# Attention turns beside an MLP stream: two turns in one round, with one stretch of projections and two groups of transposes

## The chip, the cores and the metric

The kernel runs on one core of a Trainium2 chip. The core has a matrix engine (TensorE, PE in the profile) that writes only to PSUM, a small memory of eight banks; VectorE (DVE), ScalarE (ACT) and GpSimd (POOL) for everything elementwise, of which POOL does not read PSUM in this program; and SyncE (SP), whose queue issues nearly all DMA transfers. The engines run side by side, each through its own queue in order, and wait for one another through semaphores. The metric is the device time of one execution in microseconds (us), lower is better.

## What is computed

A kernelized attention (random features), then a gated MLP on its output, all in float32:

```python
q, k, v: (8, 8, 576, 64); omega: (128, 64); x: (4608, 512); d_ff = 1536

def phi(x):
    proj = np.einsum('bhsd,md->bhsm', x, omega)
    sq = np.sum(x * x, axis=-1, keepdims=True) / 2.0
    h = proj - sq
    h = h - np.max(h, axis=-1, keepdims=True)
    return np.exp(h) / np.sqrt(m)
q_p, k_p = (phi(q_s), phi(k_s))
kv = np.einsum('bhsm,bhsd->bhmd', k_p, v)
z = np.sum(k_p, axis=2)
num = np.einsum('bhsm,bhmd->bhsd', q_p, kv)
den = np.einsum('bhsm,bhm->bhs', q_p, z)[..., None] + 1e-06
x = (num / den) with heads beside each other

g = x @ w_gate
silu = g * (1.0 / (1.0 + np.exp(-g)))
val = x @ w_val
out = silu * val @ w_out
```

## The kernel before

The attention is cut into groups of 256 rows of a pair of heads, 72 groups of q and 72 of k. A *step* holds two groups: six steps of k and k, sixty of q and k, six of q and q, 72 in all. A step passes through a pipeline of stages, one or more turns of the main loop apart:

- `st_transpose` (line 430): PE transposes the loaded rows (tile `nat`) into PSUM tile `pt`, ACT copies it to `x`; POOL squares the rows (`sq`).
- `st_project` (458): sixteen small matmuls on half of the array's rows each (`pp<-omT,x` in the profile, 64 rows by 128), into two PSUM tiles `pp`.
- `st_max` (477): DVE reduces `sq` and `pp` and works out the bias `st`; `st_exp` (497): ACT writes the features `ph` by exponentials, 128x128 at a time, and frees `pp`.
- `k_accumulate` (589): eight matmuls into `kvacc`, two turns after the projection, in two halves. When a batch's half is complete, `kv_finalize` (518) has ACT copy it to `kvr`; for batches from 4 on (`BPOOL`) PE then transposes the sums z (`zp`), ACT copies them, and they go to DRAM and back, spread over the partitions (`load_z`, 537).
- `q_transpose` (622): PE transposes q's features (`ptq`), ACT copies them to `qt`.
- For batches under 4, `q_mult` (635) multiplies with `kvr` (`po`), DVE divides (`xn`), and `q_out` (673) transposes `xn` (`xt`). From batch 4 on, the division comes first: `q_den` (550) has POOL multiply the features with z (`jk`) and DVE reduce them, `q_norm` (576) has POOL scale the features, and `q_out` does the output matmul itself (`xt<-qt,kvr`, half of the columns each). ACT (and DVE, for the first three tiles) copies `xt` out, to SBUF as a pair of high and low parts or as `xo` to DRAM.

Float32 matrix products of the MLP are made of three products of rounded parts (high and low). `stream` (772) yields the MLP's units: `g`, `v` (twelve 512-column matmuls each) and, per 128 rows, `o` (`down`, nine matmuls). Three tiles of 512 rows run through this stream in twelve visits (three tiles, four sets of three feature blocks); between two sets, new weights are fetched (`wraw`), split by ACT and POOL (`whi`, `wlo`, `split_piece`) a few units later (`land`). After a `v`, DVE multiplies with the gate (`sl`), ACT casts the result (`hh`) and POOL takes the remainder (`hl`).

The weights come in a packed form that `convert_all` (276) turns into float32 in six small steps per piece on ACT, DVE and POOL; one call of `tick` (314) issues one step, 216 in all. `behind_step` (270) keeps such work behind the newest bias of `st_max` and the newest exponential.

PSUM has eight banks: three for the MLP (`ps_moe`), two for projections (`ps_proj`), one each for `ps_att`, `ps_tr` and `kvacc`. A tile waits until the last user of its slot is done.

The main loop (line 1170) runs 76 turns. The first 25 (`EARLY`) have no MLP beside them and keep their order `CLOSE`. From turn 25 on, each turn runs the list `GROUPED` (1138): all float32 stages of PE in one group, then three `SHARE`s, then `q_norm` and `q_mult`, then three `SHARE`s. A planner has worked out beforehand how many microseconds of the MLP should be done by each turn (`course`, by its own estimates 24.4 us for a visit); at a `SHARE`, `give` takes units from the stream until its share is used up (a unit that is too long is charged to the next shares), and a part of the turn's conversion steps is issued. After the loop, the remaining six tiles go through the MLP in pairs, with nothing of the attention beside them (`pair_rounds`, line 973).

The instructions are finally put in each engine's queue by a list scheduler that goes by the order of writing but may take a later instruction when an earlier one isn't ready by its own estimate; so a queue's order can differ from the text's.

In the profile, every matmul is on line 103 and every transpose on line 107, since small helpers record them; they are told apart by tile names.

Of the kernel before, what the change touches and what calls it, by code (L numbers as in the profile page):

```python
# [24 lines left out]
def kernel(  # L25
# [295 lines left out]

    LAND = 3
    landing = []

    def load_weights(f, i):
        need(f, i)
# [2 lines left out]
    def land(upto=None):  # L329

        for t in landing:
            t[0] -= upto is None
        while landing and (landing[0][0] <= 0 or upto in [(f, i) for _, f, i, _ in landing]):
            _, f, i, raw = landing.pop(0)
            new_weights(f, i)
            with behind_step():
                split_piece(f, i, raw)
# [92 lines left out]
    def st_transpose(n):  # L430
        if n >= NS:
            return
        nat = nats.pop(n)
        pt = ps_tr(f"pt_{n}", [P, 2, G])
        for i in range(2):
            for c in range(CH):
                turned_in[:] = [
                    transpose(
                        pt[:, i, c * P : (c + 1) * P], nat[:, i, c].rearrange("p h d -> p (h d)"), ident
                    )  # L440
                ]
        x = att.tile([P, 2, G], F32, name=f"x_{n}", tag="x")

        st = att.tile([P, 4, 2, CH, 2], F32, name=f"st_{n}", tag="st", bufs=6)
# [12 lines left out]

    def st_project(n):
        if n >= NS:
            return  # L460
        x, st, sq = sts[n]

        new = ps_moe if n < EARLY and n % 2 else ps_proj
        pp = [new(f"pp{hh}_{n}", [P, 2, CH, M]) for hh in range(2)]
        for i in range(2):
            for c in range(CH):
                for hh in range(2):
                    r = slice(hh * D, (hh + 1) * D)
# [49 lines left out]
    def kv_finalize(b, a2):  # L518
        acc = kvacc.pop((b, a2))
        raw = att.tile([P, 4, VW], F32, name=f"kvr{b}_{a2}", tag="kvr", bufs=4)  # L520
        nc.scalar.copy(raw, acc)  # L521
        for j in range(2):
            kvst[b, 2 * a2 + j] = raw[:, 2 * j : 2 * j + 2, :]
        if b >= BPOOL:

            zp = ps_att(f"zp{b}_{a2}", [4, P])
            transpose(zp, raw[:, :, D], ident)
            zs = att.tile([4, P], F32, name=f"zs{b}_{a2}", tag="zs")
# [5 lines left out]
    zds = {}  # L534
    zbc = {}

    def load_z(n):
# [12 lines left out]
    def q_den(n):  # L550

        n -= JLAG
        for _, b, g, gr in slots(n, "q"):
            if b < BPOOL:
                continue
            ph = box["q", b, g].rearrange("p c (h m) -> p c h m", m=M)
            jk = att.tile([P, CH, 2, M], F32, name=f"jk{b}_{g}", tag="jx")
# [12 lines left out]
            dn = att.tile([P, 3, CH, 2], F32, name=f"dj{b}_{g}", tag="dj", bufs=6)  # L570
# [64 lines left out]
    def q_mult(n):  # L635

        n -= MLAG
        for _, b, g, gr in slots(n, "q"):
            if b >= BPOOL:
                continue  # L640
            qt = qts.pop((b, g))
            po = ps_att(f"po{b}_{g}", [P, CH, 2, VW])
            for c in range(CH):
                prs = pairs_of(gr)[c]
                w = P // len(prs) if gr is None else P
# [8 lines left out]
            dn = att.tile([P, 2, CH, 2], F32, name=f"dn{b}_{g}", tag="dn", bufs=4)  # L654
            nc.vector.tensor_scalar_add(dn[:, 0], po[:, :, :, D], EPS)
            nc.vector.reciprocal(dn[:, 1], dn[:, 0])
            xn = att.tile([P, CH, 2, D], F32, name=f"xn{b}_{g}", tag="jx")
            nc.vector.tensor_tensor(
                xn.rearrange("p c h d -> p (c h) d"),
                po[:, :, :, 0:D].rearrange("p c h d -> p (c h) d"),  # L660
# [10 lines left out]
    cols_done = [0]  # L671

    def q_out(n):
        n -= OLAG
        for i, b, g, gr in slots(n, "q"):
            po = (ps_att if n + OLAG < EARLY or i else ps_tr)(f"xt{b}_{g}", [P, G])
            first = column(b, gr)
            if b < BPOOL:
                xn = xns.pop((b, g))
# [2 lines left out]
            else:  # L682
# [3 lines left out]
                for pr, o, w in segs:  # L686
                    for hh in range(2):
                        matmul(
                            po[hh * D : (hh + 1) * D, o : o + w], kvst[b, pr][:, hh, 0:D], qt[:, hh, o : o + w],
                            start=True, stop=True, skip_group_check=True,  # L690
                        )
            j, o = tile_of(first)
            if gr is None:
                parts_ = [(po.rearrange("d (r c) -> d r c", c=RES), slice(0, NPAIR), j, o, RES)]
# [4 lines left out]
                    parts_.append((po[:, cut:G], gr[0], j + 1, 0, G - cut))  # L699
            for src, pr, j, o, w in parts_:  # L700
                if j in x_dram:
                    xo = att.tile(list(src.shape), F32, name=f"xo{b}_{g}_{j}", tag="xo", bufs=3)
                    nc.scalar.copy(xo, src)
                    nc.sync.dma_start(x_dram[j][:, pr, o : o + w], xo)
                    continue
# [7 lines left out]
        return bool(slots(n, "q"))  # L713


    def mm1(ps, wts, xs):
# [33 lines left out]

    def down(j, k_, ht, wts, next_set, tt):
        fs = sorted(ht)
        po = ps_moe(f"o{j}_{k_}_{tt}", [P, DM])
        for n, f in enumerate(fs):
            need(f, 2)
# [12 lines left out]
        if next_set is not None and tt == TILES[j][1] // P - 1:  # L768
            for f in next_set:
                load_weights(f, 2)  # L770

    def stream():

        todo = []
        for vi, (j, s_, k_) in enumerate(visits):
# [37 lines left out]
            for f in fs:  # L813
# [306 lines left out]
    def turn_next(n):  # L1120
# [17 lines left out]
    GROUPED = (  # L1138
        q_out,
        st_project,  # L1140
        q_transpose,
        lambda n: k_accumulate(n, 0),
        lambda n: k_accumulate(n, 1),
        st_max,
        st_exp,
        q_den,
        lambda n: st_transpose(n + 1),
        SHARE,
        SHARE,
        SHARE,  # L1150
        lambda n: q_norm(n + 1),
        q_mult,
        SHARE,
        SHARE,
        SHARE,
    )

    for n in range(2):
# [8 lines left out]
    warm(2, turned_in[0])  # L1167
    loaded = 3
    ends = []
    for n in range(NN):  # L1170
        if loaded <= n + LA:
            load(loaded)
            loaded += 1
# [3 lines left out]
            loaded += 1  # L1177
        if n == FIRST_RAW:
            load_raw(0)
        want = OPS * np.interp(clock[n + 1], [clock[m] for m, _ in marks], [x for _, x in marks])  # L1180
        order = CLOSE if n < EARLY else GROUPED
        left = len(order) if n < EARLY else order.count(SHARE)
        for what in order:
            with ExitStack() as es:
                if n < EARLY:
                    for ins in ends if what is st_project else ends[:1]:
                        es.enter_context(tc.issue_after(ins.ins))
                if what is not SHARE:
                    what(n)
            if n < EARLY:  # L1190
                if what is st_project:
                    ends.clear()
                ends.append(newest_pe[0])
            if what is turn_next and n < 2:
                warm(2, turned_in[0])
            if n < EARLY or what is SHARE:
                due = course[n + 1] - given[0] - debt[0]
                if due > 0:
                    give(due / left)
                for _ in range(int(np.ceil((want - ticks[0]) / left))):  # L1200
                    tick()
                left -= 1
        load_z(n)
    late.close()
    for name, pool in (
        ("win", tc.tile_pool(name="win", bufs=1)),
# [38 lines left out]
```

## Time and profile before

| what | us |
|---|---|
| median of 3 runs (1165.26 to 1167.43) | 1166.89 |
| the profiled execution | 1166.82 |
| its span, first to last instruction | 1165.0 |
| ACT busy in the span | 678.3 |
| DVE busy | 707.4 |
| POOL busy | 615.5 |
| chain of waits that ended last: share of PE | 74% |
| same chain: "issue" (no wait that the profile shows) | 2% |

A busy share says how long an engine had at least one instruction under way. Matmuls are pipelined: an instruction of 0.39 us is followed by the next after 0.23 us, so the distance from start to start is the cost, and a row "x16" of the timeline merges sixteen neighbours of the same kind. In a list of waits, "PE zp L107 <- ACT kvr L521: 2.0, 3, 1.1" means that PE, ahead of the instruction that writes zp, stood idle for 2.0 us in all, three times, at the longest 1.1, until ACT's instruction on line 521 was done.

### The profile page before, as it was taken

Reading aid. Unit: us, or ns where it says so; the run is one execution under the profiler, and the core shown is the slowest. Engines: PE = TensorE matmul, PEld = TensorE weight load, DVE = VectorE, ACT = ScalarE, POOL = GpSimd, SP = SyncE. Lnnn points to the kernel's source line nnn. Section 1 sums busy time; section 2 is a strip of 40 time slices with the busy share of each in tenths; the row PEclk is TensorE's granted clock in tenths of the full one; section 3 lists DMA queues with packets and bytes.
Section 4 is the critical chain, followed back from the end, with each engine's and each line's share of the span. In section 5 each row is a group of like instructions: output and inputs, shape, how many; then the busy total and the mean of one; then the engine's idle time right before and its main releaser. Section 6 shows DMA issues by size and latency. Waiting matters only on the chain.

```text
span 1165.0 us, 18915 instructions
## 1 busy us (share of the span) xinstructions
PE 1137.2 (98%) x6645; PEld 939.5 (81%) x6646; DVE 707.4 (61%) x1289; ACT 678.3 (58%) x1539; POOL 615.5 (53%) x559
## 2 busy tenths in 40 slices
PE   8999999999999999989999999999999999999998
PEld 6888888888878778867788778888878888888886
DVE  5787667455656656565474566665566666456654
ACT  5887886876776866757434544454544445444441
POOL 5664433344556675587245555544455543455551
PEclk9999999999999999999999999999999999999999
DMA  6764445655445642322544111124211111211103
GB/s 137 179 160 114 128 142 161 178 135 143 122 126 137 168 132 78 114 68 65 154 118 126 46 55 55 55 74 122 59 55 55 54 37 46 81 55 55 46 19 72
DMA packets 173966, 114.30 MB, mean 98 GB/s; under 512 B 125840, under 2 KB 144304, under 8 KB 173872
## 3 DMA queue, kind: packets, MB, share of 16 engines
q1 hardware_dynamic: 172528, 112.78, 35.5%
q8 instruction: 52, 0.85, 0.3%
q10 hardware_dynamic: 1344, 0.33, 0.1%
q14 instruction: 42, 0.34, 0.1%
HBM read 87.88 MB, written 25.18 MB: 97 GB/s over the span
## 4 chain that ended last, share of the span: by engine, by line
PE 74%; DVE 10%; ACT 6%; POOL 4%; DMA 3%; issue 2%; SPq 1%; ACTq 0%; POOLq 0%; DVEq 0%
PE o L103 22%; PE a L103 16%; PE c L103 8%; PE g L103 6%; PE pp L103 4%; PE v L103 4%; PE d L103 4%; PE kvacc L103 3%; ACT ph L505 3%; PE ptq L107 2%; PE po L103 2%; PE pt L107 2%; PE xt L103 1%; DVE st L490 1%; POOL wlo L264 1%
## 5 line engine op out<-in xcount | busy, mean ns | idle before, releaser
L505 ACT ACTIVATE ph<-pp,st 128x128 f32<-128x128 f32 x576 | 157.8, 386 | 26.5 <-DVE st L493 26.0
L763 DVE TENSOR_TENSOR acc<-o,acc 128x512 f32<-128x512 f32 x156 | 105.8, 684 | 94.6 <-PE o L103 94.3
L446 POOL TENSOR_TENSOR sq<-nat 128x512 f32<-128x512 f32 x72 | 78.2, 1086 | 130.5 <-DVE st L483 89.1
L950 POOL TENSOR_TENSOR wlo<-wspare,whi 128x512 fp32r<-128x512 f32 (+1 forms) x60 | 61.0, 1037 | 117.4 <-ACT whi L949 111.0
L490 DVE TENSOR_REDUCE st<-pp 128x4 f32<-128x512 f32 x144 | 92.5, 683 | 39.0 <-PE pp L103 38.7
L264 POOL TENSOR_TENSOR wlo<-wraw,whi 128x512 fp32r<-128x512 f32 x59 | 82.7, 1406 | 26.7 <-ACT whi L263 22.8
L103 PE MATMUL pp<-omT,x 64*128 64x128 f32 x1152 | 87.3, 285 | 3.2 <-ACT x L454 2.2
L103 PEld LDWEIGHTS pp<-omT,x 64*128 64x128 f32 x1152 | 72.6, 187 | 20.2 <-issue 11.2
L950 POOL TENSOR_TENSOR wlo<-s,whi 128x512 fp32r<-128x512 f32 x64 | 82.6, 1311 | 3.8 <-ACT whi L949 3.8
L1059 ACT COPY late<-a 128x512 f32<-128x512 f32 x72 | 42.2, 586 | 59.7 <-PE a L103 58.5
L103 PE MATMUL o<-whi,late 128*128 128x512 f32 x192 | 74.5, 389 | 0.0
L571 DVE TENSOR_REDUCE dj<-jk 128x4 f32<-128x512 f32 x36 | 24.6, 684 | 73.5 <-POOL jk L567 60.6
L103 PE MATMUL kvacc<-v,ph 128*128 128x65 f32 x512 | 65.9, 268 | 0.5 <-ACT kvr L521 0.5
L824 POOL TENSOR_TENSOR hl<-sl,hh 128x512 fp32r<-128x512 f32 x36 | 47.0, 1308 | 34.8 <-ACT hh L823 34.7
L103 PEld LDWEIGHTS kvacc<-v,ph 128*128 128x128 f32 x512 | 63.1, 192 | 0.8 <-ACT kvr L521 0.6
L1063 DVE TENSOR_TENSOR late<-c,late 128x512 f32<-128x512 f32 x25 | 17.3, 692 | 69.7 <-PE c L103 60.6
L103 PE MATMUL g<-xh,whi 128*128 128x512 f32 x144 | 59.4, 412 | 0.0
L103 PE MATMUL o<-whi,hh 128*128 128x512 f32 x144 | 58.5, 406 | 0.1
L303 POOL TENSOR_TENSOR wc<-st 128x512 int32<-128x512 int32 x36 | 37.5, 1042 | 39.6 <-DVE st L298 17.2
L103 PE MATMUL v<-xh,whi 128*128 128x512 f32 x144 | 57.9, 402 | 0.0
L103 PE MATMUL g<-xh,wlo 128*128 128x512 f32 x144 | 57.7, 401 | 0.0
L103 PE MATMUL g<-xl,whi 128*128 128x512 f32 x144 | 57.2, 397 | 0.0
(261 smaller groups left out, 3369.4 us busy)
## 6 DMA issues: line engine op xcount, KB each, us to landing
wraw<-wscr SPq DMA_DIRECT2D x63, 256.0 KB, 2.7
wspare<-wscr SPq DMA_DIRECT2D x60, 256.0 KB, 2.8
wscr<-wc SPq DMA_DIRECT2D x36, 256.0 KB, 2.2
out_dram<-acc SPq DMA_DIRECT2D x72, 128.0 KB, 2.4
nat<-in_k_dram SPq DMA_DIRECT2D x64, 128.0 KB, 3.0
nat<-in_q_dram SPq DMA_DIRECT2D x64, 128.0 KB, 3.1
v<-in_v_dram SPq DMA_DIRECT2D x62, 128.0 KB, 3.5
st<-in_moe_w_gate_dram SPq DMA_DIRECT2D x12, 512.0 KB, 4.1
```

The source lines that it names most:

```text
L103: newest_pe[:] = [nc.tensor.matmul(*args, **kw)]
L107: newest_pe[:] = [nc.tensor.transpose(*args, **kw)]
L264: nc.gpsimd.tensor_tensor(lo, raw, hi.bitcast(F32), op=ALU.subtract)
L303: nc.gpsimd.tensor_tensor(ui, ri, low, op=ALU.add)
L446: nc.gpsimd.tensor_tensor(sq, nat, nat, op=ALU.mult)
L490: nc.vector.tensor_reduce(st[:, 1, :, :, hh], pp[hh], axis=AX.X, op=ALU.max, negate=True)
L505: step_end["s"] = nc.scalar.activation(ph[:, c, hh * M : (hh + 1) * M], pp[hh][:, i, c, :], AF.Exp, bias=st[:, 3, i, c, hh : hh + 1], scal ...
L571: nc.vector.tensor_reduce(dn[:, 0], jk, axis=AX.X, op=ALU.add)
L763: nc.vector.tensor_tensor(a_, po, a_, op=ALU.add)
L824: nc.gpsimd.tensor_tensor(hl, h, hh.bitcast(F32), op=ALU.subtract)
L950: nc.gpsimd.tensor_tensor(lo, src_, hi.bitcast(F32), op=ALU.subtract)
L1059: newest["s"] = nc.scalar.copy(keep[name], ps)
```

## The change

From turn 25 on, the loop goes in twos. One round (`DOUBLE`) does the work of two turns, n and n+1, in this order on PE: half of `k_accumulate` of n, the output of both (`q_out_both`), the projections of n and of n+1, the other half of `k_accumulate`; six SHAREs with `q_norm` of n+1 between them; z's transposes; a half of `k_accumulate` of n+1, q's transposes of n and the rows' transposes for n+2; two SHAREs; q's transposes of n+1, the rows' transposes for n+3, the other half of `k_accumulate`; the exponentials of n+1; two SHAREs; `q_mult` of both; two SHAREs.

In the first six SHAREs of a round no conversion step is issued and no weight piece is split (`held`), unless the next unit needs it. The casts of `hh` and `hl` are no longer issued behind each `v`, but collected (`uncast`) and issued by `settle`, once in a round, or by `down` if it reads one that is still open.

PSUM slots change hands: the projections of n go to `ps_att` and `ps_tr`, those of n+1 to `ps_proj`; `xt` goes to `ps_moe`, two groups to a tile; `po` of n+1 goes to `ps_tr`; `zp` goes to `ps_moe`. Transposes `pt` stay in `ps_tr` and `ptq` in `ps_att` (a second group in `ps_tr`). In SBUF, `st` and `dj` go from six buffers to four, `xo` from three to five, `jk` and `zs` to one, and `xn` gets a tag of its own.

```diff
-        while landing and (landing[0][0] <= 0 or upto in [(f, i) for _, f, i, _ in landing]):
+        while landing and (landing[0][0] <= 0 and not held or upto in [(f, i) for _, f, i, _ in landing]):
...
-        new = ps_moe if n < EARLY and n % 2 else ps_proj
-        pp = [new(f"pp{hh}_{n}", [P, 2, CH, M]) for hh in range(2)]
+        if n < EARLY:
+            new = (ps_moe, ps_moe) if n % 2 else (ps_proj, ps_proj)
+        else:
+            new = (ps_proj, ps_proj) if (n - EARLY) % 2 else (ps_att, ps_tr)
+        pp = [new[hh](f"pp{hh}_{n}", [P, 2, CH, M]) for hh in range(2)]
...
-            zp = ps_att(f"zp{b}_{a2}", [4, P])
+            zraw[b, a2] = raw
+    def z_rows():
+        for (b, a2), raw in zraw.items():
+            zp = ps_moe(f"zp{b}_{a2}", [4, P])
             transpose(zp, raw[:, :, D], ident)
...
-            po = ps_att(f"po{b}_{g}", [P, CH, 2, VW])
+            odd = n + MLAG >= EARLY and (n + MLAG - EARLY) % 2
+            po = (ps_tr if odd else ps_att)(f"po{b}_{g}", [P, CH, 2, VW])
...
+    def q_out_both(n):
+        groups = slots(n - 1 - OLAG, "q") + slots(n - OLAG, "q")
+        at = []
+        for k_, g_ in enumerate(groups):
+            if k_ % 2 == 0:
+                two = ps_moe(f"xt{g_[1]}_{g_[2]}", [P, 2, G])
+            at.append((g_, two[:, k_ % 2]))
+        place_out(at)
...
     def down(j, k_, ht, wts, next_set, tt):
         fs = sorted(ht)
+        if any(hh is ht[f][0] for f in fs for _, hh, _ in uncast):
+            settle()
...
+    def settle():
+        for h, hh, hl in uncast:
+            with ExitStack() if late_pools else behind_step():
+                nc.scalar.copy(hh, h)
+            nc.gpsimd.tensor_tensor(hl, h, hh.bitcast(F32), op=ALU.subtract)
+        uncast.clear()
...
-                nc.scalar.copy(hh, h)
-                nc.gpsimd.tensor_tensor(hl, h, hh.bitcast(F32), op=ALU.subtract)
+                uncast.append((h, hh, hl))
+                if late_pools:
+                    settle()
...
-        lambda n: n == EARLY - 1 and q_out(n),
         lambda n: n == EARLY - 1 and q_mult(n),
+        lambda n: n == EARLY - 1 and st_transpose(n + 2),
     )
-    GROUPED = (
-        q_out, st_project, q_transpose,
...
+    DOUBLE = (
+        (lambda n: k_accumulate(n, 0), 0), (q_out_both, 0), (st_project, 0), (st_project, 1),
+        (lambda n: k_accumulate(n, 1), 0), (q_norm, 0), (st_max, 0), (st_exp, 0), (q_den, 0), (st_max, 1),
+        SHARE, SHARE, SHARE, (q_norm, 1), SHARE, SHARE, SHARE,
+        (lambda n: z_rows(), 0), (load_z, 0), (load_z, 1),
+        (lambda n: k_accumulate(n, 0), 1), (q_transpose, 0), (st_transpose, 2), SHARE, SHARE,
+        (q_transpose, 1), (st_transpose, 3), (lambda n: k_accumulate(n, 1), 1),
+        (st_exp, 1), (lambda n: settle(), 1), SHARE, SHARE,
+        (q_mult, 0), (q_mult, 1), SHARE, SHARE, (q_den, 1),
+    )
...
+    for n in range(EARLY, NN, 2):
+        loads(n)
+        loads(n + 1)
+        left, early = DOUBLE.count(SHARE), 6
+        last = min(n + 2, NN)
+        for what in DOUBLE:
+            if what is not SHARE:
+                what[0](n + what[1])
+                continue
+            held[:] = [True] if early > 0 else []
+            share(course[last] - given[0] - debt[0], ticks[0] if early > 0 else wanted(last), left)
+            left, early = left - 1, early - 1
+    held.clear()
```

`place_out` is the body of `q_out` before, cut in two loops: first all matmuls or transposes, then all copies. `loads` is the turn's start before (the loads of rows and of v), and `share` what a SHARE did before. The lists are written here with several entries to a line.

More of the change, by code (lines that the diff above doesn't have):

```diff
@@ L323 @@
     landing = []
+    held = []
     def load_weights(f, i):
@@ L442, in st_transpose @@
         x = att.tile([P, 2, G], F32, name=f"x_{n}", tag="x")
-        st = att.tile([P, 4, 2, CH, 2], F32, name=f"st_{n}", tag="st", bufs=6)
+        st = att.tile([P, 4, 2, CH, 2], F32, name=f"st_{n}", tag="st", bufs=4)
         sq = att.tile([P, 2, CH, 2, D], F32, name=f"sq_{n}", tag="sq")
@@ L524, in kv_finalize @@
         if b >= BPOOL:
-            zp = ps_att(f"zp{b}_{a2}", [4, P])
+            zraw[b, a2] = raw
+    zraw = {}
+    zds = {}
+    def z_rows():
+        for (b, a2), raw in zraw.items():
+            zp = ps_moe(f"zp{b}_{a2}", [4, P])
             transpose(zp, raw[:, :, D], ident)
-            zs = att.tile([4, P], F32, name=f"zs{b}_{a2}", tag="zs")
+            zs = att.tile([4, P], F32, name=f"zs{b}_{a2}", tag="zs", bufs=1)
             nc.scalar.copy(zs, zp)
@@ L532, in kv_finalize @@
             zds[b, a2] = zd
-    zds = {}
+        zraw.clear()
     zbc = {}
@@ L556, in q_den @@
             ph = box["q", b, g].rearrange("p c (h m) -> p c h m", m=M)
-            jk = att.tile([P, CH, 2, M], F32, name=f"jk{b}_{g}", tag="jx")
+            jk = att.tile([P, CH, 2, M], F32, name=f"jk{b}_{g}", tag="jx", bufs=1)
             if gr is None:
@@ L569, in q_den @@
                 )
-            dn = att.tile([P, 3, CH, 2], F32, name=f"dj{b}_{g}", tag="dj", bufs=6)
+            dn = att.tile([P, 3, CH, 2], F32, name=f"dj{b}_{g}", tag="dj", bufs=4)
             nc.vector.tensor_reduce(dn[:, 0], jk, axis=AX.X, op=ALU.add)
@@ L656, in q_mult @@
             nc.vector.reciprocal(dn[:, 1], dn[:, 0])
-            xn = att.tile([P, CH, 2, D], F32, name=f"xn{b}_{g}", tag="jx")
+            xn = att.tile([P, CH, 2, D], F32, name=f"xn{b}_{g}", tag="xn")
             nc.vector.tensor_tensor(
@@ L673, in q_out, with place_out @@
     def q_out(n):
-        n -= OLAG
-        for i, b, g, gr in slots(n, "q"):
-            po = (ps_att if n + OLAG < EARLY or i else ps_tr)(f"xt{b}_{g}", [P, G])
+        place_out([(g_, (ps_att if n < EARLY else ps_tr)(f"xt{g_[1]}_{g_[2]}", [P, G])) for g_ in slots(n - OLAG, "q")])
+    def q_out_both(n):
[6 more added lines that the diff above has]
+        place_out(at)
+    def place_out(at):
+        for (i, b, g, gr), po in at:
             first = column(b, gr)
@@ L691, in q_out @@
                         )
+        for (i, b, g, gr), po in at:
+            first = column(b, gr)
             j, o = tile_of(first)
@@ L701, in q_out @@
                 if j in x_dram:
-                    xo = att.tile(list(src.shape), F32, name=f"xo{b}_{g}_{j}", tag="xo", bufs=3)
+                    xo = att.tile(list(src.shape), F32, name=f"xo{b}_{g}_{j}", tag="xo", bufs=5)
                     nc.scalar.copy(xo, src)
@@ L712, in q_out @@
                 cols_done[0] = first + (RES if gr is None else G)
-        return bool(slots(n, "q"))
     def mm1(ps, wts, xs):
@@ L770, in down @@
                 load_weights(f, 2)
+    uncast = []
+    def settle():
[4 more added lines that the diff above has]
+        uncast.clear()
     def stream():
@@ L1134 @@
         q_den,
-        lambda n: n == EARLY - 1 and q_out(n),
         lambda n: n == EARLY - 1 and q_mult(n),
+        lambda n: n == EARLY - 1 and st_transpose(n + 2),
     )
-    GROUPED = (
[L1139 to L1147, printed above, removed]
+    DOUBLE = (
+        (lambda n: k_accumulate(n, 0), 0),
+        (q_out_both, 0),
+        (st_project, 0),
+        (st_project, 1),
+        (lambda n: k_accumulate(n, 1), 0),
+        (q_norm, 0),
+        (st_max, 0),
+        (st_exp, 0),
+        (q_den, 0),
+        (st_max, 1),
         SHARE,
@@ L1150 @@
         SHARE,
-        lambda n: q_norm(n + 1),
-        q_mult,
+        (q_norm, 1),
         SHARE,
@@ L1155 @@
         SHARE,
+        (lambda n: z_rows(), 0),
+        (load_z, 0),
+        (load_z, 1),
+        (lambda n: k_accumulate(n, 0), 1),
+        (q_transpose, 0),
+        (st_transpose, 2),
+        SHARE,
+        SHARE,
+        (q_transpose, 1),
+        (st_transpose, 3),
+        (lambda n: k_accumulate(n, 1), 1),
+        (st_exp, 1),
+        (lambda n: settle(), 1),
+        SHARE,
+        SHARE,
+        (q_mult, 0),
+        (q_mult, 1),
+        SHARE,
+        SHARE,
+        (q_den, 1),
     )
@@ L1169, with loads @@
     ends = []
-    for n in range(NN):
+    def loads(n):
+        nonlocal loaded
         if loaded <= n + LA:
@@ L1179, with share, wanted @@
             load_raw(0)
[L1180 to L1183, printed above, removed]
-            with ExitStack() as es:
[L1185 to L1193, printed above, removed]
+    def share(due, want, left):
+        if due > 0:
+            give(due / left)
+        for _ in range(int(np.ceil((want - ticks[0]) / left))):
+            tick()
+    def wanted(n):
+        return OPS * np.interp(clock[n], [clock[m] for m, _ in marks], [x for _, x in marks])
+    for n in range(EARLY):
+        loads(n)
+        for at, what in enumerate(CLOSE):
+            with ExitStack() as es:
+                for ins in ends if what is st_project else ends[:1]:
+                    es.enter_context(tc.issue_after(ins.ins))
+                what(n)
+            if what is st_project:
+                ends.clear()
+            ends.append(newest_pe[0])
             if what is turn_next and n < 2:
                 warm(2, turned_in[0])
[L1196 to L1202, printed above, removed]
-        load_z(n)
+            share(course[n + 1] - given[0] - debt[0], wanted(n + 1), len(CLOSE) - at)
+        load_z(n)
+    for n in range(EARLY, NN, 2):
+        loads(n)
+        loads(n + 1)
[9 more added lines that the diff above has]
+    held.clear()
     late.close()
```

## The prediction

> **What bounds the kernel now.** First the page's head and its busy shares, which say which engine to look at.
>
> ```profile
> span 1165.0 us, 18915 instructions
> PE 1137.2 (98%) x6645; PEld 939.5 (81%) x6646; DVE 707.4 (61%) x1289; ACT 678.3 (58%) x1539; POOL 615.5 (53%) x559
> ```
>
> TensorE (PE) is the bound, with 28 us idle in all, so time can come only from those gaps or from PE being busy with less. The change lies between the first MLP matmul and the last attention one; the view of tile g and the windows place that stretch.
>
> ```profile
> L103 PE MATMUL g<-xh,whi x144: 387/390/628, 111.0 to 593.1; 128*128 128x512 f32 x144
> 50.00:100.00 50.00, 48.06 (x499) 44.80 (x498) 42.61 (x122) 42.84 (x138) 33.27 (x42) 1.00 0.59 141
> 111.00:290.00 179.00, 175.98 (x1234) 148.85 (x1234) 103.86 (x233) 136.28 (x325) 73.18 (x63) 1.00 0.52 146
> 290.00:510.00 220.00, 216.62 (x1472) 173.37 (x1470) 132.77 (x277) 154.59 (x381) 142.17 (x127) 0.99 0.46 125
> 510.00:562.00 52.00, 46.11 (x296) 34.52 (x295) 30.14 (x58) 32.96 (x80) 37.89 (x34) 1.00 0.21 60
> 562.00:1165.00 603.00, 597.04 (x2640) 491.46 (x2638) 358.17 (x498) 268.77 (x479) 296.83 (x238) 1.00 0.24 68
> ```
>
> The columns are length, then busy time of PE, PE's weight loads, VectorE (DVE), ScalarE (ACT) and GpSimd (POOL), then granted clock, DMA share and GB/s. From 111 to 562 us, 51 turns of 8.8 us, PE idles 3.0 + 3.4 + 5.9 = 12.3 us; the 603 us behind it, which the change leaves alone, idle 6. No other engine is full: ACT, the next, is busy 136 of 179 us. The waits of PE in that stretch say what the 12.3 us are (total, times, longest):
>
> ```profile
> PE ptq L107 <- ACT xo L703: 2.9, 4, 2.1
> PE xt L107 <- DVE xn L658: 2.3, 2, 1.2
> PE zp L107 <- ACT kvr L521: 2.0, 3, 1.1
> PE pt L107 <- ACT qt L633: 1.9, 1, 1.9
> PE pp L103 <- ACT ph L505: 1.0, 2, 0.8
> PE pt L107 <- ACT xo L703: 0.7, 2, 0.4
> ```
>
> Most are not waits for data. They are waits for a one-buffer PSUM slot (ps_att or ps_tr) in which the last user still waits to be copied out.
>
> **The change part by part.**
>
> *Fewer stretches of projections.* Here is one turn of the later half in the order of time (start, length, engine, line, what):
>
> ```profile
> 472.54 0.39 PE L103 MATMUL g<-xh,wlo 128*128 128x512 f32 x1
> 472.85 0.65 PE L103 MATMUL xt<-qt,kvr 128*64 128x256 f32 x4
> 473.44 1.16 PE L103 MATMUL pp<-omT,x 64*128 64x128 f32 x16
> 474.53 0.66 PE L107 MATMUL ptq<-ident,ph 128*128 128x128 f32 x4
> 475.02 1.00 PE L103 MATMUL kvacc<-v,ph 128*128 128x65 f32 x8
> 475.86 0.60 PE L107 MATMUL pt<-ident,nat 128*128 128x128 f32 x4
> 476.22 0.48 PE L103 MATMUL g<-xh,whi 128*128 128x512 f32 x1
> 476.54 0.39 PE L103 MATMUL g<-xl,whi 128*128 128x512 f32 x1
> 476.77 0.39 PE L103 MATMUL g<-xh,wlo 128*128 128x512 f32 x1
> ```
>
> Matmuls overlap, so I read starts, not lengths. The sixteen projections take 474.53 - 473.44 = 1.09 us. Cutting the view's window inside that stretch gives the starts of the seventh and of the eleventh:
>
> ```profile
> 473.87 0.72 PE L103 MATMUL pp<-omT,x 64*128 64x128 f32 x10
> 474.10 0.50 PE L103 MATMUL pp<-omT,x 64*128 64x128 f32 x6
> ```
>
> Four projections in the middle take 474.10 - 473.87 = 0.23, or 0.115 us a pair (two halves of the array at once). The first six take 0.43 instead of 0.345 and the last six 0.43 instead of 0.345: 0.085 us lost going in and as much coming out, 0.17 per stretch. The instruction ahead of a stretch loses about as much: in the row of 182.54 below, two transposes take 0.31 us, where four take 0.50 (183.94 to 184.44), so 0.06. A second stretch directly behind the first thus saves about 0.25 us. Doubles 25 to 69 project twice: 23 x 0.25 = **5.7 us**. The Trainium skill (TensorEngine Tiling (Array Packing), section Key Properties) says that changing the tiling mode drains the TensorE; the trace agrees, with 0.25 us as the price here.
>
> *Output matmuls in one run (second half).* A half-width xt enters behind a g in 472.85 - 472.54 = 0.31 us, where g follows g in 0.23 (476.77 - 476.54): 0.08 once less per double, some 0.04 more on leaving. 12 doubles x 0.12 = **1.4 us**.
>
> *More edges.* The second half had one float32 group a turn, two a double; the double has three. Leaving a group costs 476.54 - 476.22 = 0.32 instead of 0.23, of which the early start of the first g gives back some (the last transpose takes under 0.1): 0.02 to 0.13 us per edge, by these rows. kvacc is also cut in halves around the projections. I take 0.12 for both, 13 doubles: **-1.6 us**. Sum of the structure: 5.7 + 1.4 - 1.6 = 5.5 us gained (bounds 4 and 7).
>
> *Waits that go.* z's transposes run after six SHAREs and in ps_moe: 2.0 us go, and with them a dip of the clock that follows the longest of the three, where g's starts are 0.43 instead of 0.23 us apart for seven matmuls (1.4 us):
>
> ```profile
> 425.42 0.63 PE L103 MATMUL g<-xh,wlo 128*128 128x512 f32 x1
> 425.85 0.63 PE L103 MATMUL g<-xh,whi 128*128 128x512 f32 x1
> ```
>
> xt moves to ps_moe, so ptq and pt no longer wait for its copy xo: 2.9 + 0.7. Projections of odd turns no longer reuse the slots of the turn just ahead: 1.0. Together 8.0 us. What stays is xn 2.3 and qt 1.9.
>
> *Waits that come.* Three places, each with the chain of rows that sets it:
>
> ```profile
> 182.54 0.38 PE L107 MATMUL xt<-ident,xn 128*128 128x128 f32 x2
> 182.85 1.16 PE L103 MATMUL pp<-omT,x 64*128 64x128 f32 x16
> 183.94 0.66 PE L107 MATMUL ptq<-ident,ph 128*128 128x128 f32 x4
> 184.44 1.00 PE L103 MATMUL kvacc<-v,ph 128*128 128x65 f32 x8
> 184.04 1.29 DVE L490 TENSOR_REDUCE st<-pp 128x4 f32<-128x512 f32 x2 [0.22 <-PE pp L103]
> 184.64 0.59 ACT L633 COPY qt<-ptq 128x512 f32<-128x512 f32 x1 [0.20 <-PE ptq L107]
> 186.46 2.18 ACT L505 ACTIVATE ph<-pp,st 128x128 f32<-128x128 f32 x8
> 226.35 0.16 DVE L655 TENSOR_SCALAR dn<-po 128x4 f32<-128x4 f32 x1 [3.71 <-PE po L103]
> ...
> 226.76 0.42 DVE L658 TENSOR_TENSOR xn<-po,dn 128x256 f32<-128x256 f32 x1
> ```
>
> (a) The even step's projections now lie in ps_att and ps_tr, where the transposes of the same double want to go. From the end of a stretch (183.94) to the last exponential (186.46 + 2.18) are 4.7 us. PE fills that with the second stretch (16 at 0.115 a pair, about 1.0), half of kvacc (0.4) and six SHAREs. The planner hands out 12 visits x 24.4 - 45 = 248 us over 51 turns, 9.7 a double, 0.81 a SHARE: 4.9 for six, at worst one unit of 2.7 (12 matmuls at 0.23). Then another half of kvacc, 0.4. So 6.7 against 4.7, and 4.5 in the worst case: covered unless ACT runs late. Without the cover it is up to 3 us a double.
> (b) Between the two groups of transposes lie two SHAREs, 1.6 us, but units come in 2.0 or 2.7, so about 9 of 26 doubles have none there. Then ptq waits for the copy qt (0.2 + 0.59), less pt's 0.36, and pt behind it for x, another 0.59, less the 0.4 of kvacc: 0.2 to 0.6, I take 0.3. 9 x 0.3 = 2.7 us.
> (c) q_mult of two steps stands two SHAREs ahead of q_out of both (before: three SHAREs). The chain from dn to the end of xn (dn's reciprocal between them) is 0.83 us per group (226.35 to 226.76 + 0.42), 1.7 for both, against 1.6 of SHAREs and 0.4 of kvacc. That holds if DVE is free. But the conversions, squeezed into the last six SHAREs, lie in DVE's queue just there: I take 0.4 in the first five doubles, 2.0 us.
>
> So 8.0 go and 4.7 come: 3.3 gained (bounds: 12 gained if nothing new comes and all goes, 13 lost under the first rival).
>
> *What costs nothing.* Casts of h wait for settle, once a double; the first product that reads them mostly stands three g units, 8 us, behind the last h, and ACT has room there. Where no settle falls between, down settles itself and PE waits for ACT's queue and POOL, some 2 to 5 us; one or two visits of ten can meet that, and I leave it to the range. Loads for two steps are issued at the double's start, the second a turn earlier, and SP holds them ahead of xo's stores. The slowest kind lands in
>
> ```profile
> v<-in_v_dram SPq DMA_DIRECT2D x62, 128.0 KB, 3.5
> ```
>
> against at least 7 us until the first use; uncovered it would be 3.5 us. The second needs a nat buffer whose last reader, POOL's square, was issued in the double before; POOL is busy only 142 of 220 us. st and dj from 6 to 4 buffers hold the at most three steps alive. One jk buffer lets POOL's second product wait for DVE's reduce; PE does not need it for six SHAREs.
>
> **Sum.** The profiled execution took 1166.82 us (span 1165.0 and 1.8 around it), 0.07 under the median of 1166.89. 1166.8 - 5.5 - 3.3 = **1158 us**.
>
> **The rivals.**
>
> *1. The slot waits win (slower).* The mechanism is (a): ps_att and ps_tr have one buffer each, and ACT's queue is first in, first out. The conversions that used to be spread over a whole turn now pile up in the last six SHAREs and spill over ahead of the exponentials. Against it: 4.7 us of chain under 6.7 of cover. For it: ACT is the fullest helper (136 of 179 us), and in the first doubles 27 steps of conversion fall into half a double. If each of 26 doubles waits 0.6 us more, 1158 + 15.6 = 1174. It decides against the change from 8.8 / 26 = 0.34 us a double.
>
> *2. The stretches don't form (same).* The order on PE is not the written one: this trace has
>
> ```profile
> 163.74 0.71 PE L103 MATMUL pp<-omT,x 64*128 64x128 f32 x6
> 164.37 0.44 PE L107 MATMUL xt<-ident,xn 128*128 128x128 f32 x2
> 164.74 0.93 PE L103 MATMUL pp<-omT,x 64*128 64x128 f32 x10
> ```
>
> where transposes that were late were put in between. If the even stretch, whose slots wait for xn, is regularly cut like this, the 5.7 us are lost and the waits only even out: 1166.8 - 0 to 1 = 1166.
>
> *3. The clock dips (slower).* Longer float32 groups without a wide matmul. The clock rows speak against it: from 50 to 100 us, before any g, it is 1.00 on float32 work alone; the one dip here followed 1.1 us of idling. If half the doubles dipped like 425.42, 13 x 1.4 = 18: 1176. The Trainium skill (TensorE: Matmul & The Clock Gate, Part 4: PE-mode transpose) holds that transposes do not count as busy for the clock gate, which would make the third group the place; no row here shows it.
>
> *4. All waits go (faster).* If the new places are covered too and qt and xn go with the slots: 1166.8 - 5.5 - 12 = 1149.
>
> **How the numbers follow.** Forecast (1154 to 1163) 0.5, rival 4 0.15, rival 2 0.18, rival 1 0.13, rival 3 0.04. A measurement of this kernel tells 0.2%, 2.3 us, from no change. Faster is the forecast and rival 4: 0.65. Same is rival 2, 0.18; slower the other two, 0.17. The range leaves out the far half of rival 4 and of the slower ones: 1149 to 1170.
>
> **What would show it.** Right: in the changed profile one stretch of projections a double (x32 in the timeline, about 2.0 us from first start to the next); zp, pp and xo gone from PE's waits; PE's idle time between the first g and the last xt near 9 us. Wrong: PE waits of ptq or pt for ph, over 0.34 us a double; pp in pieces between xt; granted clock under 0.99 in that stretch; or more than 6 us idle behind it, where I expect nothing to move.

## The result: slower, 1191.92 against 1166.62 us

The changed kernel took 1191.92 us (median of 4 runs, 1188.19 to 1193.61), the kernel before 1166.62 (4 runs) beside it: a ratio of 1.0216, 95% interval 1.0201 to 1.0231. (One of the four runs of e11 below, of 2167.16 us, was in the slow state and is left out of its median.) The forecast was 1158, its range 1149 to 1170. The page of the changed kernel, its head, its busy shares and the clock by slices:

```profile
span 1191.8 us, 18898 instructions
PE 1142.6 (96%) x6646; PEld 952.3 (80%) x6646; DVE 708.6 (59%) x1289; ACT 663.6 (56%) x1531; POOL 616.2 (52%) x559
...
PEclk9999998999998999999999999999999999999999
```

The work is the same, instruction for instruction nearly; PE's idle time rose from 1165.0 - 1137.2 = 27.8 us to 1191.8 - 1142.6 = 49.2. The clock has dips now, stretches in which PE is granted half of its clock. The windows of the changed kernel, from the first g to the last attention matmul, then behind it, then one dip:

```profile
111.00:592.40 481.40, 450.13 (x3042) 375.10 (x3040) 267.44 (x566) 312.13 (x780) 252.12 (x223) 0.97 0.43 118
592.00:1191.00 599.00, 591.20 (x2610) 485.99 (x2606) 357.99 (x498) 265.49 (x476) 298.27 (x238) 1.00 0.23 68
189.90:196.80 6.90, 6.90 (x25) 6.13 (x26) 2.10 (x8) 0.26 (x1) 0.00 (x0) 0.51 0.61 153
```

PE idles 31.3 us beside the MLP stream where it idled 12.3, and 7.8 behind it where it idled 6.0. The mean clock over the span fell from 0.997 to 0.986: at half clock in a dip, that is 2 x 0.003 x 1165 = 7 us of half clock before and 2 x 0.014 x 1191.8 = 33 now, and half of the difference, 13 us, is lost time. So 21.4 of idling and 13 of clock make 34, while the span grew by 26.8. The rest, some 7 to 8 us, is what the structure gained. (The two accounts overlap a little where PE idles at half clock.) The gain is seen directly in a round of the changed kernel (of its 23 rounds that project twice, 19 have such an unbroken stretch of 32):

```profile
353.48 1.08 PE L103 MATMUL xt<-qt,kvr 128*64 128x256 f32 x8
354.49 2.06 PE L103 MATMUL pp<-omT,x 64*128 64x128 f32 x32
356.48 0.66 PE L103 MATMUL kvacc<-v,ph 128*128 128x65 f32 x4
```

32 projections in one stretch take 356.48 - 354.49 = 1.99 us, against twice 1.09 before; the way into the second stretch comes on top. The change does what it says. What ate it are PE's waits, here those of the stretch up to the last attention matmul:

```profile
PE o L103 <- POOL hl L803: 7.1, 4, 3.8
PE po L103 <- ACT qt L644: 4.9, 3, 2.3
PE ptq L107 <- ACT qt L644: 4.2, 4, 2.4
PE ptq L107 <- ACT ph L509: 3.3, 5, 1.4
PE pt L107 <- ACT qt L644: 2.3, 1, 2.3
PE g L103 <- DVE sl L854: 2.2, 1, 2.2
PE g L103 <- ACT xo L727: 2.1, 1, 2.1
PE pt L107 <- ACT x L455: 1.6, 1, 1.6
...
PE g L103 <- POOL wlo L264: 1.0, 1, 1.0
PE xt L103 <- DVE sl L854: 0.9, 1, 0.9
```

zp, and xo ahead of the transposes, are gone as forecast. But 13.0 us wait for the copies qt and x (po, ptq, pt; 2.3 of it, pt for qt, stood at 1.9 before), 7.1 for the late hl, 5.2 for the MLP's slots (g and xt). The timeline around 188 us shows how such a wait comes about:

```profile
188.53 0.66 ACT L289 ACTIVATE wc<-st 128x512 f32<-128x512 f32 x1 [1.61 <-DMA st<-in_moe_w_out_dram]
189.10 0.57 ACT L644 COPY qt<-ptq 128x512 f32<-128x512 f32 x1
...
189.72 3.56 PE L103 MATMUL po<-kvr,qt 128*128 128x65 f32 x16 [2.21 <-ACT qt L644]
```

A conversion (L289) is at the head of ACT's queue and waits for its raw weights; the copy qt stands behind it; po wants the slot that qt empties. PE idles 2.21 us, and the sixteen po that follow take 3.56 us: the clock has halved (0.51 in the window above). At 291.48 another po waits 2.26 us, and there the conversion ahead of qt waits for POOL. At 313.38 pt waits for the copy x without ACT having been idle: ahead of x stand the gate's function (sl, L834) and, in front of that, a table load of ACT, 1.28 us:

```profile
290.29 0.67 ACT L289 ACTIVATE wc<-st 128x512 f32<-128x512 f32 x1 [2.07 <-POOL wlo L264]
...
310.96 1.28 ACT L834 ACT_TABLE_LOAD   x1
312.25 0.60 ACT L834 ACTIVATE sl<-g 128x512 f32<-128x512 f32 x1
312.75 0.58 ACT L455 COPY x<-pt 128x512 f32<-128x512 f32 x1
...
313.38 0.33 PE L107 MATMUL pt<-ident,nat 128*128 128x128 f32 x1 [1.63 <-ACT x L455]
```

Such a load also stands ahead of qt in the waits of 2.4 us at 403.49 and of 2.3 us at 554.61. The changed kernel has fewer of them beside the MLP than the kernel before (33 against 41), so their number is not what made it slower; where they stand may be part of it, and no run tests that.

The longest wait is of another kind, a cast that was issued late. Its hh is done at 458.5 us (457.91 + 0.61), and then hl stands in POOL's queue behind jk:

```profile
459.13 3.06 POOL L574 TENSOR_TENSOR jk<-ph,zt 64x256 f32<-64x256 f32 x4
...
462.28 1.26 POOL L803 TENSOR_TENSOR hl<-sl,hh 128x512 fp32r<-128x512 f32 x1
...
463.59 0.80 PE L103 MATMUL o<-whi,hl 128*128 128x512 f32 x1 [3.79 <-POOL hl L803]
```

### The profile page after: what moved, and what is told of

Its sections match the earlier page's. It is cut to its first block, busy times and chain, and to the rows that moved or that the text cites. A ratio compares the mean times of both kernels' runs of the same rounds, so it can differ in the third digit from the quotient of the medians.

```text
span 1191.8 us, 18898 instructions
## 1 busy us (share of the span) xinstructions
PE 1142.6 (96%) x6646; PEld 952.3 (80%) x6646; DVE 708.6 (59%) x1289; ACT 663.6 (56%) x1531; POOL 616.2 (52%) x559
## 4 chain that ended last, share of the span: by engine, by line
PE 45%; DVE 5%; POOL 1%; issue 1%; ACT 1%; DMA 1%; SPq 0%; POOLq 0%; DVEq 0%; ACTq 0%
PE o L103 16%; PE a L103 15%; PE c L103 8%; PE d L103 4%; PE g L103 1%; PE v L103 1%; POOL jk L578 1%; DVE late L943 1%; DMA first_b<-xs 1%; DVE s L966 0%; DVE late L1098 0%; DVE dj L582 0%; DVE first_t L928 0%; ACT ph L509 0%; POOL wlo L264 0%
## 5 line engine op out<-in xcount | busy, mean ns | idle before, releaser
L103 PE MATMUL pp<-omT,x 64*128 64x128 f32 x1152 | 80.6, 281 | 2.2 <-ACT x L455 2.2
L103 PEld LDWEIGHTS pp<-omT,x 64*128 64x128 f32 x1152 | 70.2, 187 | 12.4 <-issue 7.0
L103 PEld LDWEIGHTS kvacc<-v,ph 128*128 128x128 f32 x512 | 68.8, 193 | 6.2 <-ACT kvr L525 0.6
L103 PE MATMUL kvacc<-v,ph 128*128 128x65 f32 x512 | 72.2, 269 | 0.5 <-ACT kvr L525 0.5
L103 PE MATMUL o<-whi,hl 128*128 128x512 f32 x144 | 58.4, 406 | 7.1 <-POOL hl L803 7.1
L578 POOL TENSOR_TENSOR jk<-ph,zt 128x512 f32<-128x512 f32 x32 | 41.7, 1304 | 35.2 <-ACT ph L509 25.5
```

Source lines behind the costliest of these rows:

```text
L103: newest_pe[:] = [nc.tensor.matmul(*args, **kw)]
L578: nc.gpsimd.tensor_tensor(jk, ph, zt.rearrange("p (o h) m -> p o h m", o=1).broadcast_to([P, CH, 2, M]), op=ALU.mult)
```

## The experiments

Each result stands beside runs of the kernel before on the same chip (ratios are to these). "Idle" is PE's idle time from 111 us to the last xt, the window's length less its busy time; "clock" is the mean over the span, both of the profiled execution. The *late third* is what the change put off: conversions and splits held back to the last six SHAREs, and casts collected for settle. In the runs beside the others the kernel before took 1166.0 to 1167.0 us. Where two intervals overlap, the two runs are hardly told apart: so e1 and e6 from the change, e10 and e11 from e9, e14 from e12, and by a hair e12 from e10.

| run | us | ratio, 95% interval | idle | clock |
|---|---|---|---|---|
| before | 1166.62 | | 12.3 | 0.997 |
| after | 1191.92 | 1.0216 (1.0201-1.0231) | 31.3 | 0.986 |
| e1, all of the late third undone | 1187.18 | 1.0183 (1.0155-1.0210) | 29.5 | 0.988 |
| e2, casts at once | 1187.55 | 1.0178 (1.0159-1.0198) | 27.7 | 0.988 |
| e3, conversions spread | 1204.46 | 1.0326 (1.0295-1.0358) | 36.4 | 0.984 |
| e4, before + late third | 1167.28 | 1.0003 (0.9993-1.0012) | 11.4 | 0.997 |
| e5, second transposes in other slots | 1185.29 | 1.0165 (1.0147-1.0182) | 26.2 | 0.989 |
| e6, xt in ps_proj | 1188.42 | 1.0190 (1.0175-1.0206) | 22.5 | 0.989 |
| e7 = e5 + e6 | 1193.72 | 1.0238 (1.0223-1.0254) | 25.2 | 0.990 |
| e8 = e7 + casts at once | 1180.08 | 1.0119 (1.0101-1.0137) | 18.3 | 0.996 |
| e9 = e5 + casts at once | 1176.96 | 1.0095 (1.0078-1.0112) | 22.0 | 0.994 |
| e10 = e9 + conversions spread | 1175.10 | 1.0074 (1.0056-1.0092) | 21.1 | 0.995 |
| e11 = e9, first transposes later | 1175.99 | 1.0082 (1.0065-1.0099) | 21.2 | 0.994 |
| e12 = e10 + own scratch | 1171.16 | 1.0044 (1.0029-1.0059) | 18.9 | 0.997 |
| e13 = after + own scratch | 1185.98 | 1.0165 (1.0148-1.0182) | 27.3 | 0.989 |
| e14 = e12, first transposes later | 1172.60 | 1.0058 (1.0043-1.0073) | 20.0 | 0.995 |
| e15, before + z late | 1169.39 | 1.0021 (1.0012-1.0030) | 13.4 | 0.998 |
| e16 = e15 + xt in ps_moe | 1170.13 | 1.0029 (1.0017-1.0041) | 13.5 | 0.996 |

### Is it the late third?

The first theory, from the two waits above: conversions and casts squeezed together block ACT and POOL just where PE needs them. Its rival: the order in twos itself, with its one-buffer slots.

```diff
 e1, e2:
-                if late_pools:
-                    settle()
+                settle()
 e1, e3:
-        left, early = DOUBLE.count(SHARE), 6
+        left, early = DOUBLE.count(SHARE), 0
 e4, in the kernel before (uncast, settle and held as in the change):
+        lambda n: settle(),
         q_mult,
...
+                early = n >= EARLY and left > 3
+                held[:] = [True] if early else []
-                for _ in range(int(np.ceil((want - ticks[0]) / left))):
+                for _ in range(0 if early else int(np.ceil((want - ticks[0]) / left))):
```

Expected of e1:

> The changed kernel with its order, but conversions and splits spread over all twelve SHAREs and each cast issued right behind its v. Theory L (the late third is at fault: in the trace of the changed kernel, conversions that wait for a buffer stand in ScalarE's queue ahead of qt and xo, and late casts reach PE through POOL): about 16 us of PE's idle time and five of the six clock dips (11 us) go, 1165 us. Theory S (the one-buffer slots and the long groups themselves): 1188 to 1192 us.

Expected of e2:

> Only the casts are undone: each behind its v, conversions still in the last six SHAREs. Theory L: the waits of o for hl (7.1 us) and the dip behind the longest of them (3.4 us) go, 1181 us. Theory S: 1188 to 1192 us.

Expected of e3:

> Only the conversions and splits are undone: spread over all twelve SHAREs, casts still once a round. Theory L: the waits behind blocked conversions (five of 1.1 to 2.4 us, 10 us) and three dips (8.5 us) go, 1173 us. Theory S: 1188 to 1192 us.

Expected of e4:

> The kernel before, turn by turn as it was, with conversions and splits only in the last three of its six SHAREs and casts collected and issued once a turn. Theory L in its plain form: slower by about as much as the changed kernel, 1185 to 1192 us. If late work harms only where PE's groups wait in one-buffer slots for ScalarE: 1167 to 1173 us.

As the sole cause, the late third fell. With it gone altogether (e1), 5 of the 25 us come back, and PE still waits 9.9 us for qt and x (po, ptq, pt) where it waited 13.0; undoing the casts alone (e2) gives 4.4; and the late third on the order of before (e4) costs nothing that can be told from it. e3 fits neither theory: spread conversions with late casts are 12.5 us worse than the change, with PE's waits for hl up from 7.1 to 12.2 us and those of ptq for qt from 4.2 to 10.4. So at least a large part of the price lies in the order of twos or its slots. That is an argument by elimination; the next runs test the slots.

### Is it the slots?

```diff
 e5, e7, e8 (and e9 to e12, e14):
-        pt = ps_tr(f"pt_{n}", [P, 2, G])
+        pt = (ps_proj if n > EARLY + 1 and (n - EARLY) % 2 else ps_tr)(f"pt_{n}", [P, 2, G])
-            pt = (ps_moe if m < EARLY else ps_tr if i else ps_att)(f"ptq{b}_{g}", [P, 2, G])
+            pt = (ps_moe if m < EARLY else ps_proj if (m - EARLY) % 2 else ps_tr if i else ps_att)(f"ptq{b}_{g}", [P, 2, G])
 in DOUBLE, (st_exp, 1) moved from before settle to behind (q_norm, 1)
 e6, e7, e8:
-                two = ps_moe(f"xt{g_[1]}_{g_[2]}", [P, 2, G])
+                two = ps_proj(f"xt{g_[1]}_{g_[2]}", [P, 2, G])
 e8: the casts of e2
```

Expected of e5:

> The changed kernel, with the second group of transposes of a round in the slots of ps_proj in place of ps_att and ps_tr; so that these are free, the exponentials of n+1 are issued after the third SHARE and not after that group. Theory T (the second group and po wait for the copies qt and x of the first in the same slot, 13 us of PE's idle time, and four of the dips follow such waits, 10 us): 1170 us. If ScalarE is simply late whatever the slot: 1187 us or more.

Expected of e6:

> The changed kernel with only xt moved from the MLP's slots to ps_proj, whose last use lies half a round back. Theory X (xt and the MLP's g keep each other waiting for the three MLP slots: 5.2 us of idle time and one dip of 1.7): 1185 us. If that is nothing: 1190 to 1192 us.

Expected of e7:

> Both moves of slots together. If T and X are both right and add: 1163 us, under the kernel before. If the slots only pass the waits on: 1180 us or more.

Expected of e8:

> Both moves of slots, and the casts at once behind each v, which takes the waits of o for hl (7.1 us) and the dip behind the longest of them (3.4 us) away: 1155 us if all add up, 1187 us if the slots are not the cause.

Most of the time does not follow the waits. In e5 the 13.0 us for qt and x shrink to 0.3; the kernel gains 6.6, and PE waits instead for hl (10.0) and for the exponentials of n (6.0, ptq for ph):

```profile
PE o L103 <- POOL hl L803: 10.0, 7, 4.5
PE ptq L107 <- ACT ph L509: 6.0, 4, 2.1
...
PE pt L107 <- ACT qt L644: 0.3, 1, 0.3
```

In e6 (3.5 us faster, not clear of noise) g for xo and xt for sl are gone, 3.0 of the 5.2 us, but g for sl stays at 2.2, so that one does not hang on xt; and pp now waits 8.2 us for the copies of xt (xo 6.9, xl 1.3). The two moves together (e7) are worse than either, by a cost that is no wait: with xt and the projections in the same two slots, one of a stretch's two pp tiles comes free ahead of the other, and the scheduler issues its projections without the other's between. Two stretches of e7:

```profile
135.04 2.05 PE L103 MATMUL pp<-omT,x 64*128 64x128 f32 x24
...
240.17 2.06 PE L103 MATMUL pp<-omT,x 64*128 64x128 f32 x32
```

24 projections take as long as 32. In the records of the second stretch all 32 start in pairs, 0.007 us apart, a pair every 0.112 us; in the first, sixteen do, and the last eight start singly, also every 0.112 us. So a single one costs 0.056 us, half a pair's time, more than one in a pair. Of the 752 projections beside the MLP, 32 stand alone in the changed kernel, 204 in e6, 228 in e7 and 226 in e8: some 10 to 11 us lost in each of the three. With the casts at once (e8) the two moves come to 1180, between the two expectations.

### What is left of the order in twos

```diff
 e9: e5 with the casts of e2; e10: e9 with the spread of e1
 e11, e14, in DOUBLE: two SHAREs moved
         (q_norm, 1), (st_exp, 1), SHARE, SHARE, SHARE,
+        SHARE, SHARE,
...
         (st_transpose, 2), SHARE,
-        SHARE,
...
         (lambda n: settle(), 1), SHARE,
-        SHARE,
 e12, e13, e14:
-            u = moe.tile([P, DM], F32, name=f"wc{f}_{i}", tag="wraw", bufs=3)
+            u = att.tile([P, DM], F32, name=f"wc{f}_{i}", tag="wc", bufs=2)
 (and, for room, qt from 4 and xo from 5 buffers to 3)
```

Expected of e9:

> The second group of transposes in ps_proj (with the exponentials of n+1 after the third SHARE) and each cast at once behind its v; xt stays in the MLP's slots, since moving it tore the pairs of projections apart. If the waits of the two parts add: 10 us of idle time of o for hl and two dips behind them (5 us) go from 1185, 1170 us. If PE then only waits elsewhere: 1180 us or more.

Expected of e10:

> The same, and conversions and splits over all twelve SHAREs: with this nothing is left of the late third. If keeping the first six SHAREs free pays once the casts are out of it, slower than the run before it by 3 to 10 us (PE waits more for the exponentials of n); if the late third is what costs, faster by as much.

Expected of e11:

> Like the first of these three, with the first group of transposes after eight SHAREs in place of six, and one SHARE fewer behind each group. If the wait of the first group for the exponentials of n in its slot (10 us in PE's waits with what the profile calls issue) is what is left: 1165 us. If not: within 3 us of the first of these three.

Expected of e12:

> The run with the second slots, casts at once and everything spread, and now the conversions' scratch (wc) in two buffers of its own, not among the three that the landing weights use (xo and qt go to three buffers to make room). Theory Q (the head of ScalarE's queue is a conversion that waits for POOL to free a landing buffer, up to 5.1 us, and the exponentials stand behind it): the waits that the profile calls issue (6.1 us), g for wlo (1.3) and two dips (3.4) go, from 1175 to 1165 us. If the first group of transposes waits for the exponentials anyway: within 3 us of 1175.

Expected of e13:

> The changed kernel with nothing else than the conversions' scratch in buffers of its own (and the room made for it). Theory Q: two of its waits of po and g of 2.1 to 2.3 us and wlo's 1.0 go with the dips behind them (5 to 7 us), 1180 us. If this is not a cause by itself: 1190 us.

Expected of e14:

> The first of these three with the first group of transposes after eight SHAREs in place of six. If what is left is the wait of that group for the exponentials of n (4.1 us and the dips behind it): 1160 us, under the kernel before. If moving it only shifts the wait to the groups behind it, as one run showed: within 3 us of the first of these three.

e9 gives 15.0 us back, where e2 (4.4) and e5 (6.6) make 11.0 together; the intervals are too wide to call the excess certain. The traces fit it: as long as either wait stands, taking the other away moves PE on to it (in e5, hl from 7.1 to 10.0). Spreading the conversions as well gives 1.9 more (e10), not clear of noise: once the casts are out of it, putting conversions off has no gain that shows. Theory Q came from this stretch of e10's timeline:

```profile
427.63 1.26 POOL L264 TENSOR_TENSOR wlo<-wraw,whi 128x512 fp32r<-128x512 f32 x1
428.92 0.67 ACT L289 ACTIVATE wc<-st 128x512 f32<-128x512 f32 x1 [5.10 <-POOL wlo L264]
429.49 1.64 ACT L509 ACTIVATE ph<-pp,st 128x128 f32<-128x128 f32 x6
...
431.23 0.63 PE L107 MATMUL ptq<-ident,ph 128*128 128x128 f32 x4 [3.61 <-issue]
```

The conversion's scratch wc shares three buffers with the landing weights; the conversion sits at the head of ACT's queue for 5.10 us until POOL has split an older piece, six exponentials stand behind it, and ptq waits for the slot they free. What the profile calls "issue" here is that wait. Scratch of its own takes 3.9 us off e10 (e12) and 5.9 off the change itself (e13), some 0.4 and 0.5 of what theory Q expected (10 and 12). The waits it named went in part: in e12 issue shrinks from 6.1 to 3.8 and g for wlo stays at 1.3. No run gives the kernel before such scratch, so it is open whether it would gain as well. Moving the first group of transposes later does nothing clear of noise (e11 1.0 us faster than e9, e14 1.4 slower than e12): its wait for the exponentials shrinks, and others wait in its place (xt for qt in e11; po, o and zp in e14).

e12 is the best of the order in twos: with the late third undone, and slots of their own for the second transposes and buffers of its own for the scratch, 20.8 of the 25.3 us are back. Most of these runs land between their two expectations (e9 1177, e12 1171, e13 1186): each theory holds in part. It is still 5 us slower than the kernel before. Its waits are many small ones:

```profile
PE ptq L107 <- ACT ph L509: 4.1, 3, 2.2
PE ptq L107 <- issue: 3.8, 3, 2.2
PE o L103 <- ACT sl L834: 1.8, 1, 1.8
PE o L103 <- POOL hl L803: 1.7, 1, 1.7
PE o L103 <- DVE acc L788: 1.6, 1, 1.6
```

18.9 us of idling against 12.3 is more than the whole of why, at the same clock. What sets these waits is not settled. The place of the first group does not (e11, e14), nor the scratch alone (e12); the loads of ACT's table, seen ahead of three long waits of the changed kernel, are untested.

### Were the forecast's waits that go worth their time?

```diff
 e15, e16, in the kernel before: zraw and z_rows as in the change, and in GROUPED
         SHARE, SHARE, SHARE,
+        lambda n: z_rows(),
         lambda n: q_norm(n + 1),
 e16:
-            po = (ps_att if n + OLAG < EARLY or i else ps_tr)(f"xt{b}_{g}", [P, G])
+            po = (ps_att if n + OLAG < EARLY else ps_moe)(f"xt{b}_{g}", [P, G])
```

Expected of e15:

> The kernel before, turn by turn, with one part of the change alone: z's transposes collected, and issued in ps_moe after the third SHARE. By the forecast's own sum, 2.0 us of idle time and a dip of the clock worth 1.4 go: 1163 us. If the wait only moves, or the dip comes elsewhere: 1165 to 1167 us.

Expected of e16:

> The same, and xt of the turns beside the MLP in ps_moe as in the changed kernel. By the forecast, ptq and pt no longer wait for xo: 3.6 us more go, 1159 us. If xt and the MLP's matmuls then wait for one another in the three MLP slots, as they do in the changed kernel: 1165 us or more.

No. PE's waits in e16:

```profile
PE pp L103 <- ACT ph L505: 3.8, 3, 1.5
PE pt L107 <- ACT qt L639: 3.3, 2, 3.0
PE xt L107 <- DVE xn L664: 2.7, 5, 1.4
PE xt L103 <- DVE dj L578: 1.2, 1, 1.2
PE pt L107 <- ACT x L454: 1.0, 1, 1.0
```

zp (2.0 before; it waited for its data, kvr) and the waits of ptq and pt for xo (3.6) are gone to the last tenth. But kvacc now waits 0.6 for kvr, pp for ph has grown from 1.0 to 3.8, pt for qt from 1.9 to 3.3, and the sum is 13.5 against 12.3. Both kernels are 2 to 3 us slower than before, clear of noise. I had expected 1163 and 1159.

## Why the prediction was wrong, step by step

The forecast missed by 34 us. It expected PE to idle near 9 us beside the MLP and a dip less; PE idled 31.3, some 22 more, and the clock cost 13 where 1.4 should have been gained; the structure gave back about 2. So the step that failed by size is the account of new waits, in "Waits that come" and "What costs nothing", with no price for the dips that follow them.

- **Fewer stretches, more edges: 5.5 us gained (4 to 7). Right.** The change forms its stretches, and what is left of the account after idling and clock is 7 to 8 us, a little more. Rival 2 (the stretches don't form) did not happen.
- **"Waits that go", 8.0 us: failed.** The forecast read the list of waits as a list of gains. The named waits went; e15 and e16 show for zp and xo (5.6 us of idling), with no other part of the change, that the time did not go with them. The list names who released PE last, not what PE would have waited for next.
- **"Waits that come", 4.7 us: failed by size and in kind.** Place (b), the second group of transposes behind the copies of the first, was priced at nine waits of 0.3, 2.7 us; ptq for qt and pt for x were five waits of 1.2, 5.8 us. po, which I had left out of that chain, waited another 4.9 for qt. I had put ACT's copy at its own length plus 0.2 and forgotten what may stand ahead of it in the queue: a conversion waiting for a DMA (1.61 us at 188.53) or for POOL (2.07 us at 290.29, 5.10 in e10), or a table load. Place (a), ptq for ph, covered by the forecast, was 3.3 us, and 6.0 to 8.3 in e5 and e9; the forecast's own worst case of cover, 4.5 us, was already under the chain's 4.7. Place (c), xn, was forecast with 2.0 more and shrank to 0.3.
- **"What costs nothing": wrong for the casts.** I left down's late settle to the range; PE's waits for hl were 7.1 us. And xt in the MLP's slots was counted as a gain only; g and xt waited 3.0 us there that e6, with xt elsewhere, does not have.
- **Rival 1 (slot waits win), given 0.13 and 1174: the right mechanism in part, half the size (15.6 of 34 us).** It blamed the piled-up conversions; e4 and e1 show that the pile is not the price by itself. As far as the runs show, it is the slots and the late casts together (e9), with what stands ahead of the copies in ACT's queue (e12, e13).
- **Rival 3 (the clock), given 0.04 and 1176: the clock did cost 13 us, but not by the path named.** Each of the six dips begins in an idle of PE of 2.09 us or more or within 1.5 us behind it; nowhere else beside the MLP is the clock below full. The clock should not have stood as a rival beside rival 1 but as its multiplier.

## What to carry to other kernels

A wait in the list is not a gain in waiting: ask what PE would wait for next if it came there 2 us earlier, and count only what all helpers are early for; a wait that another stands in for may pay only when both go. When work is grouped on the bound engine, the copies that empty its slots come in bursts too: look at what can stand at the head of the copying engine's queue (a DMA, another engine's release, a table load), not at the copy's own length. And an idle of PE of over 2 us is to be priced with the dip behind it: 44 of 56 had one in these runs.

## What the hardware showed that I had not expected

All 67 half-clock stretches between 111 and 1150 us, in all eighteen profiles, last 3.41 us or a multiple of it (6.83, once 10.24), and each begins in an idle of PE of 0.8 us or more or at most 2.2 us behind its end. Counting PE's idles in the same stretch of these profiles, with a half-clock stretch that begins within 7 us of the idle's start: of 133 between 0.8 and 1.6 us, 20 have one; of 51 between 1.6 and 2.4 us, 27; of 33 longer ones, 29. In the changed kernel all six (30.7 us together) go with idles of 2.09 to 3.79 us. A dip of 3.41 us costs up to 1.7, so that a wait of 2.2 us like the one at 189.72 cost 2.2 and, with 6.83 us of half clock behind it, up to 3.4 more.

The Trainium skill (TensorE: Matmul & The Clock Gate, the table under Why this matters for your kernels) warns of idle gaps over about 3 us. These runs agree on the kind and put the point lower: 2.4 us is nearly always enough, 1.1 us sometimes (the one dip of the kernel before). What the Trainium skill says of transposes (TensorE: Matmul & The Clock Gate, Part 4: PE-mode transpose), which the forecast named beside its third rival, finds no support here: in the changed kernel sixteen transposes (ptq, pt) and eight kvacc in a row ran at clock 1.00.

```profile
344.86:347.44 2.58, 2.58 (x25) 2.52 (x24) 2.54 (x5) 1.50 (x4) 1.88 (x2) 1.00 0.95 268
```

Whether a longer row of transposes alone would lower the clock is not tested.
